# Batch 0's second feature half moves to the end of round two in a cross-attention and SERF feed-forward kernel

## The chip, the cores and the metric

The kernel runs on one core of one Trainium2 chip. Its time is the device time in microseconds (us) of one execution. Before the change, three runs took 704.97, 705.04 and 706.51 us; the median is 705.04 us. Besides these runs there is one profiled execution, with a record of each instruction on each engine.

The engines are named as in the profile: PE is TensorE (matrix products), PEld its loading of stationary operands, DVE is VectorE, ACT is ScalarE, POOL is GpSimd, and SP is SyncE, which only issues transfers here. A name such as SPq or POOLq is the DMA queue of that engine. "ACT copy" or "DVE copy" below means a copy of a result from PSUM, where TensorE leaves it, to SBUF.

## The reference, cut to what matters

```python
B, H, S, Ns, D = 8, 8, 512, 32, 64          # x: (B, H, S, D), state: (B, H, Ns, D)
d_model, d_ff = 512, 2048

scores  = x @ state^T / sqrt(D);  a  = softmax(scores)     # (B, H, S, Ns)
xread   = a @ state                                        # each token reads the states
scores2 = state @ x^T / sqrt(D);  a2 = softmax(scores2)    # (B, H, Ns, S)
sread   = a2 @ x                                           # each state reads the tokens
rows    = concat([xread, sread], axis=2) -> (B * (S + Ns), H * D) = (4352, 512)

h   = rows @ w_in                                          # w_in  (512, 2048)
g   = h * erf(softplus(h))
out = g @ w_out                                            # w_out (2048, 512)
```

The inputs x and state are float32. The two weight matrices arrive as float64; the chip sees them as pairs of 32-bit words, and the kernel makes float32 of them with two passes on ScalarE and three instructions on VectorE for each piece.

## The kernel before, in words

**Features and batches.** The 2048 features of d_ff are 16 blocks of 128; four blocks are a group, so there are four groups, and two groups are a feature half. Half 0 is groups 0 and 1, half 1 is groups 2 and 3. A batch has 512 token rows (four tiles of 128 rows) and 32 state rows.

**Mixed product.** Since xread is a times state, the first layer is computed as a times (state @ w_in). The product state @ w_in of a batch for one group is called mixed here: `mixed_part` (L600, products in L613) for batch 0, `mixed` (L1130, products in L1138) for the others. Its results are copied from PSUM to tiles named `m`.

**Batch 0 with plain products.** At the start, only batch 0 is worked on, while the weights arrive. It goes through all four groups with ordinary products: `first` (L617, product L624) makes h, `second` (L626, product L631) accumulates the output rows in four PSUM banks over all 16 blocks. Softplus and erf run on ScalarE (L661, L664), the multiplication by h on VectorE (L666). The weights come from SP's queue in pieces (`weight`, L140): w_in pieces of two blocks and w_out pieces of two blocks, 1 MB of float64 each, 8 of each matrix. They go through a ring of three buffers named `raw`, and are converted by ScalarE (L167, L169) and VectorE (L172, L173, L174). Pieces of w_in for half 1 are laid in a part of `ring` and stored to DRAM (`kept_in`) from there by `kept`. The order of all these steps is a list written out by hand, `order0` (L758), with the steps' short names: p201 is the second product of group 2, row tile 0, block 1; i4v0 is the first VectorE step of w_in's piece 4. `lead` and `warm` (L191, L193) put products whose result is not used ahead of others.

**Strassen products for the other batches.** Batches 1 to 7 use products of Strassen's kind with seven multiplications in place of eight. `first_product` (L1223, product L1237) makes h for one half: two column parts of seven products, 14 in all, each of four records in the profile. `serf` (L1267) does softplus and erf on ScalarE and the multiplication on VectorE (L1277). `sums_a` (L1284, L1288) makes sums of blocks of g, and `sums_w` (L1299, L429) differences of blocks of w_out, four instructions for a half. `second_product` (L1308, L1321) multiplies them by seven products. `twice_product` (L1411, product L1508) applies the scheme at two levels, 49 products of four records; `sums_b` (L1367, L1383) makes its weight sums. `sums_y` (L1170) makes the sums of attention weights that the first product needs; `keep_y` and `bring_y` store them in DRAM and bring them back.

**Rounds.** Round one makes half 0 of batches 1 to 7, with `second_product` for batches 1 to 5 and `twice_product` for 6 and 7, and writes the partial output rows. In it the attention of the following batches is computed (`attend` L980, `read` L1089, `turn_read` L1112). State rows of all batches are done together (`first_states`, `second_states`). Round two makes half 1 of batches 1 to 7 with `twice_product`, and adds to the rows already in DRAM by accumulating transfers on GpSimd's queue (L1556). The very last unit (half 1 of batch 7) instead reads the stored rows back into tiles, adds its blocks to them in SBUF (`join`, L1568) and stores the sums from SP's queue (`store`, L1572).

**The weights between the rounds.** The weight sums of half 1 (`sums_w(1, ...)`) are made in batch 2's unit of round one. `keep_w` (L1403) then stores w_out's half 1 and its three sums in DRAM, four transfers on SP's queue, since `sums_b` for half 0 is going to overwrite them before batch 6; `bring_w` brings them back before round two.

**What sets the order.** From batch 1 on, each instruction or short series of instructions is an `op` (L796) with its engine, a planned cost, a planned time, and the regions that it reads and writes. `ORDER` fixes for each engine the order of its ops. `emit` (L919) goes through them on the plan's clock and issues them; `in_order` (L82) then ties each engine to that order. So every engine, and every queue so tied, runs its list strictly in order: an instruction that waits holds up all that follow on its engine. In part one `in_order` covers TensorE, VectorE, ScalarE and SP; from batch 1 on, TensorE, VectorE and ScalarE.

## Time and profile before

| | |
|---|---|
| median of three runs | 705.04 us |
| span of the profiled execution | 702.9 us |
| TensorE busy | 694.6 us (99%) |
| VectorE busy | 571.8 us (81%) |
| ScalarE busy | 469.3 us (67%) |
| GpSimd busy | 58.9 us (8%) |
| granted TensorE clock | 1.00 in each window read below |
| bytes moved by DMA | 85.54 MB, mean 122 GB/s |

The span runs from the first to the last event of the profiled execution on the core. It lies 2.1 us under the median of the three runs; what is outside the span is not in the trace. A busy time is the sum over an engine's instructions, without overlap counted twice. In the lists of groups, a row names line, engine, operation, output and input tiles and the number of records, then the busy time and the mean duration in ns of one record. Successive records overlap a little, so the distance from one start to the next is shorter than the mean duration. A float32 matrix product appears in the profile as two records for each weight block, so 64 plain products of L631 for batch 0 (4 row tiles by 16 blocks) are 128 records. In the rows of waits, the figures are the total time waited, the number of waits, and the longest, in us.

### The profile page before, as it was taken

The page shows a single profiled execution, that of the slowest core. Times are in us where ns is not written, and L with a number is a line of the kernel's source. Part 1 is how long each engine was busy: PE and PEld are TensorE (multiplying, and loading weights), DVE is VectorE, ACT ScalarE, POOL GpSimd, SP SyncE. Part 2 cuts the span into 40 slices and gives each one's busy share as a digit, 9 for nine tenths or more (in the row PEclk, how much of TensorE's full clock was granted, in tenths as well). Part 3 has the DMA queues.
Part 4 walks back from the last instruction along what each step waited for, and adds up shares of the span by engine and source line. Part 5 has one row for each costly group of instructions (what it writes and reads, how often), then busy time and mean ns, then how long its engine had stood idle before and what let it go on. Part 6 is the DMA issues. An engine that isn't in the chain of part 4 may idle for free.

```text
span 702.9 us, 12986 instructions
## 1 busy us (share of the span) xinstructions
PE 694.6 (99%) x5039; PEld 565.4 (80%) x5039; DVE 571.8 (81%) x930; ACT 469.3 (67%) x812; POOL 58.9 (8%) x54
## 2 busy tenths in 40 slices
PE   8999999999999999999999999999999999999997
PEld 7444346687878778787999998798989898989997
DVE  6997887999979788696969753896979587778997
ACT  5999898949576655838473455846585756666842
POOL 0000000000000000000001000102021221212322
PEclk9999999999999999999999999999999999999999
DMA  8869582845648746352234514405152663435665
GB/s 261 260 194 252 191 192 46 201 86 108 179 85 259 198 81 201 55 173 53 93 98 120 161 58 165 98 31 96 17 98 33 111 75 69 60 42 65 104 94 106
DMA packets 159886, 85.54 MB, mean 122 GB/s; under 512 B 123728, under 2 KB 149328, under 8 KB 159056
## 3 DMA queue, kind: packets, MB, share of 16 engines
q1 hardware_dynamic: 146224, 71.59, 36.5%
q0 software_dynamic: 13056, 12.59, 14.3%
q8 instruction: 40, 0.66, 0.4%
q10 hardware_dynamic: 544, 0.52, 0.2%
q14 instruction: 22, 0.18, 0.1%
HBM read 46.27 MB, written 34.73 MB: 115 GB/s over the span
## 4 chain that ended last, share of the span: by engine, by line
PE 94%; DVE 4%; issue 0%; ACT 0%; DVEq 0%; ACTq 0%
PE o L1508 28%; PE o L1321 17%; PE h L1237 17%; PE o L631 8%; PE at L1237 7%; PE o L1725 3%; PE h L1676 3%; PE h L624 2%; PE at L624 2%; PE h L1138 2%; PE at L1138 2%; PE at L1676 1%; PE at L1100 1%; PE h L997 1%; PE at L613 1%; DVE ring L1568 1%
## 5 line engine op out<-in xcount | busy, mean ns | idle before, releaser
L1249 ACT COPY ring<-h 128x512 f32<-128x512 f32 x112 | 64.7, 586 | 84.3 <-PE h L1237 81.2
L1237 PE MATMUL h<-aT,m 128*128 128x256 f32 x336 | 85.1, 380 | 0.0
L1277 DVE TENSOR_TENSOR ring<-ring 128x1024 f32<-128x1024 f32 (+1 forms) x60 | 68.6, 1146 | 14.0 <-ACT ring L1274 13.4
L1321 PE MATMUL o<-w_out,ring 128*128 128x256 f32 x320 | 77.7, 383 | 0.0
L1321 PEld LDWEIGHTS o<-w_out,ring 128*128 128x128 f32 x320 | 59.6, 190 | 15.9 <-issue 5.9
L1259 ACT ACTIVATE ring<-ring 128x512 f32<-128x512 f32 x112 | 66.7, 631 | 6.6 <-PE o L1321 2.1
L1237 PEld LDWEIGHTS h<-aT,m 128*128 128x128 f32 x336 | 61.8, 190 | 10.4 <-ACT ring L1249 0.8
L1288 DVE TENSOR_TENSOR ring<-ring 128x1024 f32<-128x1024 f32 x56 | 67.8, 1217 | 0.3
L631 PE MATMUL o<-w_out,ring 128*128 128x512 f32 x128 | 59.7, 599 | 0.0
L1508 PE MATMUL o<-w_out,w_in 128*128 128x128 f32 x448 | 59.6, 275 | 0.0
L1274 ACT ACTIVATE ring<-ring 128x1024 f32<-128x1024 f32 (+1 forms) x60 | 59.0, 1004 | 0.2
L1321 PE MATMUL o<-raw,ring 128*128 128x256 f32 x240 | 58.9, 381 | 0.1
L1508 PE MATMUL o<-w_out,ring 128*128 128x128 f32 x432 | 58.8, 276 | 0.0
L1508 PEld LDWEIGHTS o<-w_out,ring 128*128 128x128 f32 x432 | 54.1, 192 | 4.2 <-issue 1.7
L1508 PEld LDWEIGHTS o<-w_out,w_in 128*128 128x128 f32 x448 | 56.0, 192 | 1.7 <-issue 0.8
L1556 POOL DMA_DIRECT2D out_dram<-oo x14 | 17.0, 1213 | 448.5 <-ACT o L1529 360.8
L1321 PEld LDWEIGHTS o<-raw,ring 128*128 128x128 f32 x240 | 45.3, 190 | 9.5 <-issue 2.5
L631 PEld LDWEIGHTS o<-w_out,ring 128*128 128x128 f32 x128 | 23.7, 190 | 27.6 <-issue 26.2
L1508 PE MATMUL o<-raw,ring 128*128 128x128 f32 x324 | 44.7, 276 | 0.0
L1508 PEld LDWEIGHTS o<-raw,ring 128*128 128x128 f32 x324 | 41.3, 192 | 2.4 <-issue 1.7
L1251 DVE TENSOR_TENSOR ring<-ring,at 128x512 f32<-128x512 f32 x28 | 19.1, 684 | 23.5 <-ACT ring L1249 21.8
L1508 PE MATMUL o<-raw,xT 128*128 128x128 f32 x288 | 37.3, 275 | 0.0
(289 smaller groups left out, 1391.5 us busy)
## 6 DMA issues: line engine op xcount, KB each, us to landing
raw<-in_moe_w_in_dram SPq DMA_DIRECT2D x16, 512.0 KB, 4.8
raw<-in_moe_w_out_dram SPq DMA_DIRECT2D x8, 1024.0 KB, 5.3
xq<-in_x_dram SPq DMA_DIRECT2D x112, 64.0 KB, 2.5
x<-in_x_dram SPq DMA_DIRECT2D x56, 128.0 KB, 3.2
out_dram<-oo SPq DMA_DIRECT2D x10, 512.0 KB, 3.7
kept_a<-aT SPq DMA_DIRECT2D x7, 512.0 KB, 3.2
aT<-kept_a SPq DMA_DIRECT2D x7, 512.0 KB, 4.6
out_dram<-oo POOLq DMA_DIRECT2D x14, 256.0 KB, 4.4
```

The source lines that it names most:

```text
L624: nc.tensor.matmul(out=h_t[g, i], lhsT=m_t[0, g][:, e, P * i:P * i + P], rhs=aT[0][:, e], start=start, stop=not start)
L631: nc.tensor.matmul(out=acc[r], lhsT=gT[g][:, i, P * r:P * r + P], rhs=w_out[:, GF * g + i, :], start=(made_of[r] == 1), stop=(made_of[r] = ...
L1138: nc.tensor.matmul(out=bank(names[e])[q, :], lhsT=st[r, b, q], rhs=of_group[2 * u + j][r, :, i, :], start=True, stop=True)
L1237: nc.tensor.matmul(out=out_[:, i], lhsT=x_[:, q:q + P], rhs=y_, start=(start and i == 0), stop=(i == 1), skip_group_check=not start)
L1249: op(ACT, 0.5, t, lambda: nc.scalar.copy(out_(), view(bank(name))), [name], w)
L1259: op(ACT, 0.53, t, lambda: nc.scalar.activation(out=part(splane, k), in_=part(hplane, k), func=ACTF.Softplus), area(hplane, ks=[k], os=[o] ...
L1274: op(ACT, 0.085 + 0.875 * share, at + n, lambda s_=s_: nc.scalar.activation(out=s_, in_=s_, func=ACTF.Erf), [], area(splane, ks=[k], os=os ...
L1277: op(DVE, 0.065 + 1.075 * share, at + n + 1, lambda s_=s_, h_=h_: tt(s_, s_, h_, op=ALU.mult), area(hplane, ks=[k], os=os), area(splane, k ...
L1288: op(DVE, 1.14, at + k, lambda k=k, x_=x_, y_=y_, how=how: tt(get("h", k), get(*x_), get(*y_), op=how), area(v[x_[0]], ks=[x_[1]]) + area( ...
L1321: nc.tensor.matmul(out=view(name)[:, h], lhsT=lhs[:, i, :], rhs=weight_of[n]()[:, u, i, :], start=(start and h == 0 and i == 0), stop=(h = ...
L1508: nc.tensor.matmul(out=out_[:, Q2 * k:Q2 * k + Q2], lhsT=lhs[:, k, i], rhs=rhs[:, i], start=first, stop=(k == len(ns) - 1 and i == 1), ski ...
L1676: nc.tensor.matmul(out=bank(bk)[:, P * i:P * i + P], lhsT=x_[:, i, k], rhs=y_[:, k], start=(start and i == 0 and k == 0), stop=(i == GF - ...
```

## The change

Batch 0 no longer does all of its features at the start.

1. **Only half 0 of batch 0 at the start.** Batch 0's steps become ops of the planner (`begin0`, `mixed0`, `first0`, `serf0`, `second0`, `put0`), for groups 0 and 1 only. `order0` and its helpers go. Batch 0's four partial row tiles are stored by `put0`, from GpSimd's queue.
2. **Half 1 of batch 0 as the last unit of round two.** Round two runs over batches 1 to 7 and then 0. The new last unit uses `first_product` and `twice_product` as the others do, with its own `sums_y`, `keep_y`, `bring_y` and `mixed`.
3. **Weights of half 1 staged in round one.** SP's queue fetches only the first eight pieces of 1 MB. The blocks of half 1 are fetched in 16 stages (`stage`), one block of 512 KB each, alternately of w_in and w_out, by GpSimd's queue into halves of the three `raw` buffers; each is converted with the same five instructions, half as wide. A converted block of w_in is stored to `kept_in`, by GpSimd's queue.
4. **Weight sums and their store.** `sums_w(1)` moves from batch 2's unit to that of batch 5 (`TWICE - 1`), and `keep_w` goes from SP's queue to GpSimd's.
5. **Copies.** Of batch 0's copies from PSUM, ten named in `BY_VECTOR` are on VectorE, and all others on ScalarE.
6. **The last block.** In the last unit, the output block whose products come last is no longer copied to a temporary and joined. Each of its results is added straight from PSUM to the tile that holds the rows read back (`into`), and the block is stored in three parts.
7. **Orders.** `ORDER` is new for all engines and also has GpSimd's and SP's queues for the whole kernel; `in_order` covers all five. The planned time of batch 1's first unit (`BASE`) is 66 in place of 24.

```diff
-    def in_order(begun, engines=(nc.tensor, nc.vector, nc.scalar, nc.sync)):
+    def in_order(begun, engines=(nc.tensor, nc.vector, nc.scalar, nc.sync, nc.gpsimd)):
...
+    BY_VECTOR = set("""
+        x2 st s01 m010 m011 m020 m021 u0 u1 m120""".split())
...
+    def spare_products(name, n, at):
+        op(PE, 0.112 * n, at, lambda: warm(bank(name)[:, 0:P], n), [], [name])
...
+            spare_products("o%d" % g, 3 if g else 14, 12.6 + 5 * g)
...
+    def fetch_in(f, k, h, at, late=False):
+        how, on = late_load if late else ((SP, 0.5), nc.sync)
+        op(*how, at, lambda: on.dma_start(
+            out=half(k, h).rearrange("p (a b) -> p a b", a=NK),
+            in_=moe_w_in[:, P * f:P * f + P].rearrange("(k p) f -> p k f", p=P).bitcast(U32)),
+           [("out0", 1)] * late, RAW(k, [h]), land=9.0 * late, pipe=1.42 * (not late))
+
+    late_load = (GP, 2.0), nc.gpsimd
+
+    def fetch_out(f, k, h, at):
+        op(GP, 1.4, at, lambda: nc.gpsimd.dma_start(
+            out=half(k, h), in_=moe_w_out[P * f:P * f + P].bitcast(U32)),
+           [("out0", 1)], RAW(k, [h]), land=8.0)
...
+    def second0(g, r, i, at):
+
+        def go():
+            made_of[r] += 1
+            nc.tensor.matmul(out=bank("o%d" % r), lhsT=gT[g][:, i, P * r:P * r + P],
+                             rhs=w_out[:, GF * g + i, :], start=(made_of[r] == 1),
+                             stop=(made_of[r] == NF // 2))
...
+    def put0(r, at):
...
+        op(ACT, 0.48, at, lambda: nc.scalar.copy(ot(), bank("o%d" % r)), [],
+           ["oacc%d" % r, "ot%d" % (r % 2)])
+        rows = out[0:S].rearrange("(p c) e -> c p e", p=P)
+        op(GP, 1.2, at + 1, lambda: nc.gpsimd.dma_start(out=rows[r], in_=ot()),
+           ["ot%d" % (r % 2)], [("out0", r)], land=4.0)
...
     def keep_w(at):
-        op(SP, 2.4, at, lambda: [nc.sync.dma_start(out=k, in_=t) for t, k in weights_of(1)],
+        op(GP, 5.6, at, lambda: [nc.gpsimd.dma_start(out=k, in_=t) for t, k in weights_of(1)],
+           W_of(1), ["kept_w"], land=18.0)
...
+            if final is not None and ns == (3,):
+                join_others()
+
+                def into(frm, h, q, t, region=region, of_bank=of_bank):
+                    to = mine(0, 1)[:, h, Q2 * q:Q2 * q + Q2]
+                    op(DVE, 0.2, t, lambda: tt(to, to, region[frm](), op=ALU.add),
+                       [of_bank[frm]], area(final, us=[0], ks=[2 + h], os=[q]))
+
+                copy = add = into
...
-            join(0, 1, R3, at + 22)
-            store(0, 1, at + 22)
...
+        if final is not None:
+            for h, qs in (1, slice(0, 2)), (0, slice(0, 1)), (0, slice(1, 2)):
+                cols = slice(Q2 * qs.start, Q2 * qs.stop)
+                op(SP, 0.4, at + 26, lambda h=h, cols=cols: nc.sync.dma_start(
+                    out=quad(0, 1)[:, h, cols], in_=mine(0, 1)[:, h, cols]),
+                   area(final, us=[0], ks=[2 + h], os=range(qs.start, qs.stop)), [], land=2.2)
+            return
...
-    U, BASE = 40.0, 24.0
+    U, BASE = 40.0, 66.0
...
+    def stage(n, at):
+        f, k, e = NF // 2 + n // 2, n % 3, n // 2 % 2
+        if n % 2:
+            fetch_out(f, k, 1, at)
+            convert(("o", f), half(k, 1), w_out[:, f], RAW(k, [1]), [("Wo", f)], at + 5)
+        else:
+            fetch_in(f, k, 1, at, True)
+            convert(("i", f), half(k, 1), mt(3)[:, e], RAW(k, [1]), [("mS", 1, e)], at + 5)
+            op(GP, 1.4, at + 10, lambda: nc.gpsimd.dma_start(
+                out=kept_in[:, f - NF // 2], in_=mt(3)[:, e]), [("mS", 1, e)],
+               [("kin", f - NF // 2)], land=6.0)
+
+    for n in range(NF):
+        stage(n, BASE + 8 + 8 * n)
...
-            if b == 2:
-                sums_w(1, base + 20, 1, 2, 4, 3)
-                keep_w(base + 30)
+            if b == TWICE - 1:
+                sums_w(1, base + 5, 1, 2, 4, 3)
+                keep_w(base + 12)
...
+    turns = [*range(1, B), 0]
...
     emit()
-    in_order(begun, [nc.tensor, nc.vector, nc.scalar])
+    in_order(begun)
```

## The prediction

> **What bounds the kernel now.** I read the page's engine totals first, then its slices, its chain of waits, the list of what TensorE (PE) waited for, and a table of 20 us windows.
>
> ```profile
> span 702.9 us, 12986 instructions
> PE 694.6 (99%) x5039; PEld 565.4 (80%) x5039; DVE 571.8 (81%) x930; ACT 469.3 (67%) x812; POOL 58.9 (8%) x54
> PE   8999999999999999999999999999999999999997
> DVE  6997887999979788696969753896979587778997
> PE 94%; DVE 4%; issue 0%; ACT 0%; DVEq 0%; ACTq 0%
> PE o L531 <- DVE ring L553: 1.1, 1, 1.1
> PE o L193 <- PEq L1915: 0.8, 1, 0.8
> PE at L1113 <- ACT sT L1116: 0.7, 1, 0.7
> PE o L485 <- DMA x<-in_x_dram: 0.4, 1, 0.4
> PE h L613 <- DVE w_in L174: 0.4, 1, 0.4
> PE at L1138 <- DVE ring L1255: 0.2, 1, 0.2
> 20.00:40.00 20.00, 20.00 (x82) 8.73 (x82) 18.78 (x29) 19.87 (x24) 0.00 (x0) 1.00 0.75 214
> 140.00:160.00 20.00, 20.00 (x163) 16.42 (x162) 18.98 (x32) 9.87 (x19) 0.00 (x0) 1.00 0.52 93
> ```
>
> TensorE is the bound: 99% busy, 94% of the chain, and its six waits sum to 3.6 us, all before 140 us. The granted clock is 1.00 in every window, so only TensorE's work and its waits can move the time. VectorE (DVE) is the engine that comes next: in the windows its column (the third busy one) reads 18.78 and 18.98 of 20. So a change that takes TensorE's work out of the start may find VectorE there.
>
> **What leaves TensorE.** Groups 2 and 3 of batch 0 go, which were plain products.
>
> ```profile
> 27.78 10.30 PE o L631 x24
> 19.21 3.52 PE h L624 x8
> 135.82 6.04 PE o L1321 x28
> 357.37 2.68 PE o L1508 x24
> 168.59 1.02 PE h L1138 x16
> ```
>
> These pieces of the chain give the pace: 10.30/24 = 0.429 us for a record at L631, 3.52/8 = 0.44 at L624 (0.43 in the longer runs), 6.04/28 = 0.216 for a 256-wide one, 2.68/24 = 0.112 at L1508, 1.02 for a mixed product. Half of L631's 128 records is 64 x 0.429 = 27.5; 32 of L624's 64 at 0.43 are 13.7; four mixed products of 0.6 are 2.4. That is 43.6 us away. The new unit adds 14 first products of 4 records (56 x 0.216 = 12.1), 49 two-level ones of 4 (196 x 0.112 = 21.9) and two mixed (2.0): 36.0. TensorE is relieved of 7.6 us.
>
> **The end.** In the timeline before, TensorE ends at 698.26, the last sum in L1523 runs to 698.89, and the join in L1568 from 698.99 to 699.68; then the store lands. Adding straight from PSUM leaves the join out: 0.8 us. The three stores instead of one can cost this again (0 to 0.8); I take 0.8, since the stores' issues lie on an empty SP queue.
>
> So the span is 702.9 - 3.6 - 7.6 - 0.8 + L = 690.9 + L, where L is all the time that TensorE will wait. The profiled execution's span lies 2.1 us under the median of the runs, 705.04, so the time is 693.0 + L. It breaks even at L = 12.
>
> **L: what VectorE has to do before the first Strassen products.** I lay the new order out by rows. A conversion of a piece is L172, L173, L174: their starts lie 0.60, 1.14 and 1.14 apart, 2.9 in all; a half piece 1.5. Other 512-wide instructions start 0.60 apart, 1024-wide ones 1.15. The first multiplication (L1277) that batch 1's second product needs is the 127th instruction in VectorE's new order; the 126 ahead are: 7 whole pieces, the first in two parts and three staged halves (27.8), attention of batches 1 and 2 (33 instructions, 19.0), batch 0's softmax (8.5), 8 multiplications L666 (4.8), four weight sums (4.6), copies from PSUM (3.9), sums of L1170 (2.7), mixed sums (2.4), three multiplications (1.8), two additions (1.2): 76.7. VectorE first has data at 5.9 (its wait for L485), so 82.6. TensorE's work ahead of the same product: warm-up and lead products 8.9 (22 leads at 3.39/14 = 0.24), attention 12.3, mixed 2.6 + 2.0, first products of batch 0 13.8, second 31 x 0.858 = 26.6, batch 1's first 12 x 0.863 = 10.4, from 0.8: 77.4. The gap is 5.2; the same account at batch 3's second product gives 5.4, and it closes after about 240 us.
>
> On top of it: VectorE's idle time at the head, where scores, the 14 leads and the softmax stand in one row. Before, 0-20 us had 6.7 idle, 0.8 beyond the first 5.9; walking the new order, 3.7. I take 3.0, near the upper end, since fewer conversions are at hand to fill it. Then gaps between instructions: the best window before was 97% busy (19.42 of 20), 3% of 77 is 2.3. Against it, my TensorE prices sum to 678.3 for the whole new queue where 694.6 - 7.6 = 687.0 is due, 1.3%, 1.0 at this place. L = 5.2 + 3.0 + 2.3 - 1.0 = 9.5, and the time 702.5; the case spans 700 to 706 (L 7 to 13: no idle at the head below, gaps up to batch 3 above).
>
> **What I cost at nothing, and its cover.** ScalarE (ACT): 8 conversions of 2 x 1.05 go (16.8) and table loads fall from 28 to about 15 (13 x 1.28), while some 5 us of copies and 1.2 per staged half come; it was 87% busy to 143 us and gets less. SP's queue loses 12 loads of weights, and the 2 stores of kept_in, 4 of keep_w and 4 of batch 0's rows go to GpSimd (POOL) or are replaced there: nothing on SP is later. GpSimd gets 16 loads, 8 stores, 4 of keep_w, 4 of rows: 32 issues at 1.20 to 1.46 us (its rows at L1556), 38 to 47 us in some 150 that were empty. Without that room each would delay the next load. The 16 staged conversions (1.5 each on VectorE, about 75 to 205 us) stand for 8 whole ones (23.2) that were done before 105 us; those that fall before the place in question are in the sum. The weight sums for half 1 (4 x 1.15) move from batch 2 to batch 5, as much work as before; keep_w must have landed before sums_b overwrites: VectorE has 22.7 us of work between. On SP keep_w took 6.6 to 8.1; GpSimd's 256 KB took 4.4 where SP's took 2.2, so 8.1 to 16.2: hidden. Behind it on GpSimd's queue wait only accumulating stores of outputs, which TensorE does not need. The extra unit in round two runs at VectorE's 80%.
>
> **A rule on GpSimd's loads.** While VectorE was 19.01 of 20 busy (680 to 700), GpSimd's issues stayed at 1.20 to 1.46 us. Only L172-like instructions (0.60) could stand in a load's way. The Trainium skill, page SBUF — State Buffer, section SBUF: two separate sides, says that such a load needs descriptors that GpSimd writes, and that it is locked out while VectorE runs a two-port instruction; it measures 620 ns growing to 3100. By this each staged load would be some 2.5 us later, an estimate from that page; hidden again while stages are 8 us apart. The trace here shows no such growth.
>
> **Rivals.**
> *VectorE idles as before* (slower). In its first 100 us it was busy 82.7, so 11.4 idle after the 5.9. It waited there for ScalarE's erf results (L666, 5.7) and copies (L1251, 2.7) and for products (L613, 3.5). If the new order keeps all of it, L = 5.2 + 11.4 - 1.0 = 15.6, 708.6 us. It decides from L = 14.1, that is 9.9 us of idle before batch 1's second product. Against it: fewer table loads on ScalarE and copies taken off VectorE's list.
> *A staged weight is late.* Conversions stand at fixed places in VectorE's order, so a piece not landed stops the multiplications behind it and TensorE after them. Loads on GpSimd's queue stand behind stores of kept_in that wait for VectorE. One whole landing of 5.8 us at VectorE's head gives L = 15.3, 708.3 us. Three buffers and 8 us a stage speak against it.
> *VectorE keeps up.* TensorE's own pace hides the gap (b1's products interleaved with batch 0's): L 4 to 7, say 5.5, 698.5 us. For it: TensorE waited 3.6 only before, with VectorE at 95%.
> *The unit is not cheaper.* If the last unit waits for its own sums, as no other unit follows to fill TensorE, the 7.6 is gone in part: 3 to 5 us, 706. The last unit before had no such wait (20.00 in every window to 680, 18.24 in the last).
>
> **How the numbers follow.** No change is within 0.3%, 2.1 us, about what can be told here: 702.9 to 707.2. My case (702.5): 0.55, of it 0.30 below 702.9 and 0.25 within. VectorE keeps up: 0.10, faster. VectorE idles: 0.20, slower. A late weight: 0.10, of it 0.07 slower. Unit not cheaper: 0.05, within. Faster 0.40, same 0.33, slower 0.27. My case's own range is 700 to 706; for 8 in 10 with both signs I take 698 to 709.
>
> **What would show it.** TensorE busy about 687; L1508 records 196 more, L631's half. TensorE's waits sum to about 9.5, nearly all before 160 us and on VectorE's L1277-like multiplications or on first-product sums, not on a DMA. VectorE over 93% busy from 20 to 160 us. In the tail no 0.69 join after the last product. Wrong: a long wait of VectorE for raw from GpSimd's queue, waits of TensorE after 240 us, or VectorE under 88% in the first 100 us while TensorE waits.

## The result, and the profile after

The changed kernel took 723.13 us (median of four runs, 719.11 to 726.7) beside 705.0 before: a ratio of 1.025, with a 95% interval of 1.021 to 1.029. It is slower by 18 us where 702.5 was forecast, and lies outside the range of 698 to 709. The profiled execution is the shortest of the four, with a span of 717.3 us. Its trace thus explains 14.4 us of the difference; what the longer executions add is taken up with the experiments. A run over 1.5% above the fastest run of its kernel is left out of the ratios; there is one, the longest of the kernel with ten leads at the head.

The page of the changed kernel: the engines' totals, TensorE's granted clock in 40 slices, and the chain of waits.

```profile
PE 698.8 (97%) x5163; PEld 581.6 (81%) x5163; DVE 593.4 (83%) x989; ACT 471.9 (66%) x850; POOL 85.7 (12%) x93
PEclk9899998999999999999999999999999999999999
PE 82%; DVE 4%; SPq 4%; DMA 1%; ACT 1%; issue 1%; DVEq 0%; ACTq 0%
```

TensorE's share of the chain has fallen from 94 to 82%, and SP's queue and the DMA, which had no place in it, have come in. The granted clock has two dents, in slices 2 and 7. These are the waits of TensorE over 1.1 us: what waited and its line, for what, us in total, times, longest.

```profile
PE h L684 <- DVE xq L676: 3.6, 1, 3.6
PE h L580 <- ACT m L161: 2.1, 1, 2.1
PE at L114 <- POOL ident masks.py:199: 1.4, 1, 1.4
PE o L1003 <- DVE ring L959: 1.3, 1, 1.3
PE o L438 <- DVE ring L463: 1.3, 1, 1.3
PE h L820 <- ACT ring L931: 1.2, 1, 1.2
```

And four windows of it around the two dents: from and to, length, busy time of TensorE, its weight loads, VectorE, ScalarE and GpSimd with their instructions, the granted clock, the DMA share and GB/s.

```profile
20.00:24.00 4.00, 2.75 (x9) 1.86 (x10) 3.86 (x10) 3.26 (x7) 0.00 (x0) 0.50 0.59 105
24.00:28.00 4.00, 4.00 (x22) 1.38 (x20) 3.84 (x6) 3.98 (x6) 0.00 (x0) 0.68 0.37 88
104.00:108.00 4.00, 1.59 (x12) 0.76 (x16) 2.40 (x5) 0.00 (x0) 0.00 (x0) 0.63 0.91 198
108.00:112.00 4.00, 4.00 (x20) 2.13 (x7) 3.74 (x8) 2.43 (x5) 0.55 (x1) 0.51 0.64 123
```

All waits of TensorE sum to 12.9 us (3.6 before). Its busy time is 698.8 us (694.6 before), and the time behind its last product 5.2 (4.6 before): these three make up 14.1 of the 14.4 us. The granted clock is 0.50 to 0.68 in these four windows; it was 1.00 in each that the prediction read. Summed over windows of 2 us, busy time times the missing part of the clock is 5.4 us; this work at half speed is part of the busy time.

The largest wait, L684, is that of the scores of batch 3 for its tokens (`xq`). The chain of waits (start, length) shows what it hung on; L93 is the load of xq.

```profile
89.15 5.76 SPq L93
...
95.58 2.90 SPq L93
...
102.84 2.56 DMA xq<-in_x_dram
...
105.60 0.72 DVE xq L676
106.32 0.09 issue
106.41 3.07 PE h L684 x16
```

SP's rows of the timeline show its list up to there (start, length; L768 loads x, L754 transfers the attention weights; two stores lie between them and xq):

```profile
62.56 10.47 SPq L768 DMA_DIRECT2D x<-in_x_dram  x8
73.13 11.46 SPq L754 DMA_DIRECT2D sc<-xT  x16
...
85.81 17.52 SPq L93 DMA_DIRECT2D xq<-in_x_dram  x16
```

And GpSimd's rows of the same timeline, with its idle time before and what ended it in brackets:

```profile
85.43 0.55 POOL L533 DMA_DIRECT2D raw<-in_moe_w_out_dram  x1 [21.16 <-DVE m L550]
86.49 1.09 POOL L1529 DMA_DIRECT2D kept_in<-m  x2 [0.51 <-DVE m L550]
87.58 0.54 POOL L657 DMA_DIRECT2D out_dram<-ot  x1
88.11 0.76 POOL L525 DMA_DIRECT2D raw<-in_moe_w_in_dram  x1
88.86 0.54 POOL L533 DMA_DIRECT2D raw<-in_moe_w_out_dram  x1
90.17 0.55 POOL L657 DMA_DIRECT2D out_dram<-ot  x1 [0.77 <-ACT ot L654]
```

SP's list had no idle stretch from 53 to 118 us; 4.8 us of this time are waits of x's transfers (L768) until TensorE is done with the tokens before. The 16 transfers of xq took 17.52 us to issue, with 5.76 and 2.90 us in two single issues; the same 16 took 10.70 before. SP's rows of the kernel before at that place in its list:

```profile
98.55 4.34 SPq L76 DMA_DIRECT2D x<-in_x_dram  x8
110.60 10.57 SPq L361 DMA_DIRECT2D sc<-xT  x16
...
123.41 10.70 SPq L105 DMA_DIRECT2D xq<-in_x_dram  x16
```

There the list stood idle from 103 to 111 us. In the changed kernel GpSimd let out seven transfers in just the stretch of the 17.52 us, 2.5 MB (three loads and two stores of rows at 512 and 256 KB, two stores of `kept_in` at 256 KB), after it had stood 21 us for VectorE to free a buffer.

The tail, from the timeline: TensorE's last products, VectorE's last sum, and SP's last stores.

```profile
711.40 0.68 PE L1239 MATMUL o<-w_out,w_in 128*128 128x128 f32 x4
712.22 0.48 DVE L1264 TENSOR_TENSOR ring<-ring,o 128x128 f32<-128x128 f32 x2
712.11 1.24 SPq L1175 DMA_DIRECT2D out_dram<-ring  x2
713.39 1.10 SPq L1288 DMA_DIRECT2D out_dram<-ring  x2
```

From TensorE's end to the end of the span are 5.2 us, where 4.6 were measured before and 3.8 forecast. The join is gone, but the last stores stand on SP's list behind two others that are ready at the same moment.

### The profile page after: what moved, and what is told of

The parts are those of the page before. It is cut to its first block, busy times and chain, and to the rows that moved or that the text cites. A ratio compares the mean times of both kernels' runs of the same rounds, so it can differ in the third digit from the quotient of the medians.

```text
span 717.3 us, 13372 instructions
## 1 busy us (share of the span) xinstructions
PE 698.8 (97%) x5163; PEld 581.6 (81%) x5163; DVE 593.4 (83%) x989; ACT 471.9 (66%) x850; POOL 85.7 (12%) x93
## 4 chain that ended last, share of the span: by engine, by line
PE 82%; DVE 4%; SPq 4%; DMA 1%; ACT 1%; issue 1%; DVEq 0%; ACTq 0%
PE o L1239 30%; PE h L919 17%; PE o L1003 15%; PE at L919 7%; PE o L1422 3%; PE h L1373 3%; SPq L93 2%; PE h L820 2%; PE at L820 2%; SPq L754 1%; PE h L684 1%; PE at L1373 1%; PE at L782 1%; DVE ring L970 1%; PE o L622 1%
## 5 line engine op out<-in xcount | busy, mean ns | idle before, releaser
L919 PE MATMUL h<-aT,m 128*128 128x256 f32 x360 | 92.1, 382 | 0.1
L941 ACT ACTIVATE ring<-ring 128x512 f32<-128x512 f32 x120 | 72.3, 631 | 10.9 <-PE o L1003 2.6
L1003 PE MATMUL o<-w_out,ring 128*128 128x256 f32 x320 | 77.6, 383 | 1.3 <-DVE ring L959 1.3
L1003 PEld LDWEIGHTS o<-w_out,ring 128*128 128x128 f32 x320 | 60.1, 191 | 16.5 <-issue 3.0
L1239 PE MATMUL o<-w_out,w_in 128*128 128x128 f32 x512 | 69.2, 276 | 0.0
L1239 PEld LDWEIGHTS o<-w_out,w_in 128*128 128x128 f32 x512 | 64.5, 192 | 1.9 <-issue 0.3
L1239 PE MATMUL o<-w_out,ring 128*128 128x128 f32 x480 | 65.1, 276 | 0.0
L1239 PEld LDWEIGHTS o<-w_out,ring 128*128 128x128 f32 x480 | 60.5, 192 | 4.3 <-issue 0.8
L1159 POOL DMA_DIRECT2D out_dram<-oo x16 | 24.4, 1585 | 151.1 <-ACT ring L956 115.0
L1239 PEld LDWEIGHTS o<-raw,xT 128*128 128x128 f32 x320 | 38.8, 192 | 2.1 <-ACT o L1270 1.7
L622 PE MATMUL o<-w_out,ring 128*128 128x512 f32 x64 | 31.0, 607 | 0.1
L919 PE MATMUL at<-sy,sx 128*128 128x256 f32 x120 | 31.0, 381 | 0.0
```

The costliest lines, as they stand in the source:

```text
L622: nc.tensor.matmul(out=bank("o%d" % r), lhsT=gT[g][:, i, P * r:P * r + P], rhs=w_out[:, GF * g + i, :], start=(made_of[r] == 1), stop=(mad ...
L919: nc.tensor.matmul(out=out_[:, i], lhsT=x_[:, q:q + P], rhs=y_, start=(start and i == 0), stop=(i == 1), skip_group_check=not start)
L941: op(ACT, 0.53, t, lambda: nc.scalar.activation(out=part(splane, k), in_=part(hplane, k), func=ACTF.Softplus), area(hplane, ks=[k], os=[o] ...
L1003: nc.tensor.matmul(out=view(name)[:, h], lhsT=lhs[:, i, :], rhs=weight_of[n]()[:, u, i, :], start=(start and h == 0 and i == 0), stop=(h = ...
L1159: op(GP, 1.2, t, lambda: nc.gpsimd.dma_start(out=quad(r, c), in_=one(v), accum_op=ALU.add), every(*v), [("out", b, r, c)], land=6.0)
L1239: nc.tensor.matmul(out=out_[:, Q2 * k:Q2 * k + Q2], lhsT=lhs[:, k, i], rhs=rhs[:, i], start=first, stop=(k == len(ns) - 1 and i == 1), ski ...
```

## The experiments

Ratios are to the kernel before on the same chip, each with its 95% interval; its median was 704.84 to 704.95 us on each of these chips. A figure in us as measured is the median of a kernel's runs, and a wait or a clock is that of its one trace. Theory A in what follows: GpSimd's staged transfers collide with SP's, SP's list in strict order passes the delay on, and TensorE's waits bring its clock down.

**Quarter of the staged loads.**

```diff
-            out=half(k, h).rearrange("p (a b) -> p a b", a=NK),
+            out=half(k, h).rearrange("p (a b) -> p a b", a=NK)[:, 0:1 if late else NK],
...
-            out=half(k, h), in_=moe_w_out[P * f:P * f + P].bitcast(U32)),
+            out=half(k, h)[:, 0:d_model // 2],
+            in_=moe_w_out[P * f:P * f + P, 0:d_model // 4].bitcast(U32)),
```

> Each of the 16 staged weight loads moves a quarter of its bytes (128 KB in place of 512 KB); the order, the waits and the conversions stay, so half 1 of the weights is not what it should be. Theory A (the transfers collide): at 85 to 96 us GpSimd's loads and stores fill the DMA engines and SP's issue of batch 3's xq is held (one issue took 5.76 us, another 2.90), VectorE's transpose and TensorE's scores wait, and the clock halves behind it. It expects the 16 issues to take about 10.5 us in place of 17.5, TensorE's wait of 3.6 us at the scores and the second halving of the clock to be gone, and 6 to 9 us less. Theory B (VectorE's and SP's own lists are too long there, whatever the load): the wait stays at 3 to 4 us and the time within 2 us.

Measured: 713.57 us, 1.0119 (1.0104 to 1.0134), 9.6 less than the changed kernel. Each staged load moves a quarter of its bytes here. SP's row of the timeline:

```profile
82.21 12.71 SPq L93 DMA_DIRECT2D xq<-in_x_dram  x16
```

And the two windows of the second dent:

```profile
104.00:108.00 4.00, 4.00 (x20) 3.54 (x19) 3.97 (x10) 3.40 (x7) 0.27 (x1) 1.00 0.50 115
108.00:112.00 4.00, 4.00 (x20) 3.21 (x18) 3.90 (x6) 3.43 (x6) 0.00 (x0) 1.00 0.28 45
```

The 16 issues took 12.71 us, not quite the 10.5 that was expected, and TensorE does not wait for xq. The bytes of the staged loads, not their order or their conversions, made the wait at 103 us and the second dent. The wait of 1.2 us at 257 us of the changed kernel stands here at 250 us with 2.2, and a clock down behind it.

**No staged conversions.** The three VectorE instructions and the second ScalarE pass of the staged conversions are left out.

```diff
+        short = len(key) == 2 and words.shape[1] < 2 * 2 * d_model
...
-        op(DVE, 0.6 if full else 0.35, at + 0.6, lambda: nc.vector.tensor_scalar(
+        op(DVE, 0.6 if full else 0.35, at + 0.6, lambda: short or nc.vector.tensor_scalar(
...
-        op(ACT, 1.05 if full else 0.6, at + 0.5, lambda: nc.scalar.activation(
+        op(ACT, 1.05 if full else 0.6, at + 0.5, lambda: short or nc.scalar.activation(
...
-        op(DVE, 1.15 if full else 0.6, at + 1, lambda: tt(d, d, lo, op=ALU.add),
+        op(DVE, 1.15 if full else 0.6, at + 1, lambda: short or tt(d, d, lo, op=ALU.add),
...
-        op(DVE, 1.15 if full else 0.6, at + 2, lambda: nc.vector.scalar_tensor_tensor(
+        op(DVE, 1.15 if full else 0.6, at + 2, lambda: short or nc.vector.scalar_tensor_tensor(
```

> The three VectorE instructions and the second ScalarE pass of each of the 16 staged conversions are left out (so half 1 of the weights is not what it should be); loads and stores stay. It takes 24.5 us of VectorE and 9.6 us of ScalarE from 75 to 210 us. Theory A (transfers): the wait for batch 3's xq stays, VectorE has 4.6 us less before batch 1's second product, 2 to 5 us less time in all. Theory B (VectorE bounds the whole start): the lag falls by all that TensorE waits for there, 8 us or more.

Measured: 719.76 us, 1.0204 (1.0187 to 1.0221), 3.4 less in the median, with runs that overlap, for 24 us of VectorE's work. Of TensorE's waits in this kernel the longest is new, and the chain of waits shows what it hung on:

```profile
PE at L784 <- DMA sc<-xT: 8.3, 1, 8.3
```

```profile
84.09 9.50 DMA sc<-xT
```

TensorE now waits 8.3 us for the attention weights of batch 1, which SP issues from 73.27 to 85.55. The last of these transfers took 9.50 us to land, where the median of them took 2.6: GpSimd let out three staged loads, two stores of `kept_in` and one of rows from 81 to 85 us, and the DMA share read 0.92 and 1.06 in the two windows from 82 to 86 us. So the collision came back at another transfer. The wait for batch 3's xq, which theory A expected to stay, is gone. The gain is within the 2 to 5 us of theory A, and VectorE's sum alone does not bound the start.

**The staged loads on SP's queue.**

```diff
-    late_load = (GP, 2.0), nc.gpsimd
+    late_load = (GP, 2.0), nc.sync
...
-        op(GP, 1.4, at, lambda: nc.gpsimd.dma_start(
+        op(GP, 1.4, at, lambda: nc.sync.dma_start(
```

> The 16 staged loads go out from SP's queue in place of GpSimd's, at the place in the list that the plan's clock gives them; all else as in the changed kernel. Theory A (what hurts is the load on the DMA engines, and SP's list in strict order with it): no better, since the same bytes move at the same time and SP's list gets 16 more entries that wait for VectorE to free a buffer; 0 to 20 us slower than the changed kernel, 720 to 740. Theory C (GpSimd's own queue is slow, as its descriptors are): the loads land sooner and 3 us or more are won, below 719.

Measured: 723.15 us, 1.0258 (1.0238 to 1.0277), as the changed kernel. The long waits moved (6.1 us for VectorE's L933, ending at 177 us, and 3.8 for ScalarE at about 88), none was won. The equal time is made of two things. The staged loads went out at other times, xq's 16 issues took 13.04 us, and TensorE did not wait for xq at 103 us. In exchange a staged load stood on SP's list behind the 16 transfers of a later xq until 166.7 us; ScalarE waited 7.0 us for it to land, and VectorE 6.2 us for ScalarE. From issue to landing, the median of the staged w_out loads is 5.2 us in place of 6.0. So GpSimd's queue as such is not what costs the 18 us, but how much a queue of its own is worth is not shown.

**A burst in the kernel before.** The collision by itself, in two kernels.

```diff
+    def burst():
+        for k in range(5):
+            nc.gpsimd.dma_start(out=spare[:, k], in_=aT[1].rearrange("p e s -> p (e s)"))
```

> The kernel before, with five more stores on GpSimd's queue: batch 1's attention weights (512 KB, five times, 2.6 MB) to a spare tensor in DRAM as soon as they are made, at about 120 us, beside SP's 16 transfers of batch 3's xq, whose issues took 10.70 us. Nothing reads the copies. Theory A (transfers collide, and that alone slows SP's list): the 16 issues take 14 to 18 us. If the kernel before has room in SP's list there, as its idle stretch of 14 us before them suggests, the time stays within 1 us of 705; if not, up to 4 us more. Otherwise: issues at 10.5 to 11 us.

Measured: 705.94 us, 1.0018 (1.0008 to 1.0027). The five stores went out at 107.9 us, not at 120, and did not meet xq, whose issues took 10.36 us. The attention weights, issued from 111 us on, took 12.51 us in place of 10.57. In the second kernel the five copies of 512 KB go from DRAM to DRAM: they read the stored weights, and so start when that store has landed.

```diff
+            nc.gpsimd.dma_start(out=spare[:, k], in_=kept_a[1].rearrange("p e s -> p (e s)"))
...
+    op(GP, 6.0, 0, burst, ["kept1"], [])
```

> The kernel before, with five copies of 512 KB on GpSimd's queue from the store of batch 1's attention weights to a spare tensor, DRAM to DRAM, which can start when that store has landed, at 126 to 127 us, beside SP's 16 transfers of batch 3's xq (10.4 to 10.7 us for the issues). If colliding transfers alone slow SP's issue, it takes 14 us or more, as in the changed kernel (17.5 with 2.6 MB beside it). The time: as before within 1 us where SP's list has room, 2 to 5 us more where not. If they do not collide, 10.4 to 11 us.

Measured: 712.04 us, 1.0103 (1.0086 to 1.012). GpSimd's and SP's rows of the timeline:

```profile
124.44 2.78 POOL L1903 DMA_DIRECT2D spare<-kept_a  x5 [123.14 <-DMA kept_a<-aT]
```

```profile
124.13 16.46 SPq L105 DMA_DIRECT2D xq<-in_x_dram  x16
```

And TensorE's longest wait:

```profile
PE at L1100 <- DMA m<-xT: 2.6, 1, 2.6
```

With 2.5 MB beside them the 16 issues took 16.46 us where they took 10.70. This was passed on along SP's list to the attention weights behind them, for which TensorE waited 2.6 us; the clock then read 0.82 and 0.76 in the two windows of 4 us after 156 us. One burst cost the kernel before, with its idle stretches on SP's list, 7.2 us: more than the expected 2 to 5. So added transfers alone, with order and work as before, slow SP's list and TensorE behind it.

**Rows of half 0 from GpSimd's queue.** The wait of 1.2 us at L820 (257 us) had the same shape: SP's store of a row block (L1023) stood behind xq of batch 7, whose 16 issues took 18.09 us beside `keep_w`'s 3.5 MB on GpSimd's queue, and ScalarE waited 3.2 us for its landing.

```diff
-            op(SP, 0.4, t, lambda: nc.sync.dma_start(out=rows[r], in_=oo()[:, r]),
+            op(SP, 0.4, t, lambda: nc.gpsimd.dma_start(out=rows[r], in_=oo()[:, r]),
```

> The stores of half 0's rows of batches 1 to 5 (512 KB each) go out from GpSimd's queue in place of SP's, where one stood at 251 us behind the 16 transfers of batch 7's xq (18.1 us for the issues) and 8 of x, with ScalarE waiting 3.2 us for its landing and TensorE 1.25. Theory A: this wait is gone, 1 to 2 us less (3 to 5 in executions where the clock halves there); the wait at 103 us stays. Otherwise: unchanged within 1 us.

Measured: 718.2 us (717.19 to 718.35), 1.0185 (1.0168 to 1.0202). There is no wait of TensorE from 230 to 300 us. The median is 4.9 lower, and the runs differ by 1.2 us where those of the changed kernel differ by 7.6. Three of the other kernels with SP's list as in the change (spare products in the wait, order of the head, short conversion, all told below) had, in their profiled executions of 722.2 to 726.0 us, a further wait of 4.0 to 4.4 us at about 175 us: for a VectorE multiplication that stands on VectorE's list behind the transposition of a later xq. This xq landed late, issued behind two row stores and beside three staged transfers. That the longer runs of the changed kernel have this wait too is likely, but they left no trace.

**All of it small.** Staged loads a quarter, the store and fetch between the rounds a quarter, rows from GpSimd's queue; of these edits, that of the store:

```diff
...
-        op(GP, 5.6, at, lambda: [nc.gpsimd.dma_start(out=k, in_=t) for t, k in weights_of(1)],
+        op(GP, 5.6, at, lambda: [nc.gpsimd.dma_start(out=k[:, 0:k.shape[-1] // 4],
+                                                     in_=t[:, 0:t.shape[-1] // 4])
+                                 for t, k in weights_of(1)],
...
```

> All that collides is made small or taken off SP's list: staged weight loads a quarter, the store and the fetch of half 1's weights between the rounds (keep_w, bring_w) a quarter, and half 0's rows of batches 1 to 5 go out from GpSimd's queue; so half 1 of the weights is not what it should be. Theory A (the collisions and what hangs on them): no wait of TensorE over 1.5 us after 30 us and no halved clock there; what is left is the head with its halved clock (7 us), VectorE's lag before 91 us (6) and the tail (1.4): 708 to 711 us. Theory B (another cause after 100 us): 713 or more.

Measured: 710.31 us, 1.0076 (1.0061 to 1.0091), within the expected 708 to 711. Its longest waits:

```profile
PE h L582 <- ACT m L161: 2.1, 1, 2.1
PE at L114 <- POOL ident masks.py:199: 1.4, 1, 1.4
PE o L438 <- DVE ring L463: 1.3, 1, 1.3
```

All three lie in the first 23 us. So 12.8 of the 18 us are the transfers and what hangs on them. Counting TensorE's records one by one shows where: against the same record of the changed kernel this one is 0.3 us ahead at 97 us, 8.2 at 107.5 (115.7 there), and 9.7 at 354. Nearly all is won at the one wait for xq with its clock, and the rest after 230 us, where the wait at 257 us lay. This kernel still is 5.4 us slower than before. Its waits are 7.1 us (3.6 before), all of them ahead of 110 us, its halved clock costs 2.8, and its tail is 0.6 us longer.

**Spare products in the wait for the scores.**

```diff
+    op(PE, 0.24 * 14, 0, lambda: warm(bank("h0")[:, 0:P], 14), [], [])
```

> Fourteen spare products (3.4 us) stand ahead of batch 3's scores, where TensorE waits 3.6 us for its xq. They cost nothing if they run in the wait. Theory A (a wait of TensorE of this length brings the clock down to 0.50 for some 6 us): the clock stays at 1.00 at 105 to 112 us and 2.5 to 3 us are won. Theory B (the clock comes down for another reason): clock 0.50 there as before, no gain.

```profile
104.00:108.00 4.00, 3.43 (x31) 2.45 (x33) 2.13 (x4) 0.13 (x1) 0.00 (x0) 1.00 0.89 188
108.00:112.00 4.00, 4.00 (x25) 2.83 (x16) 3.93 (x8) 3.02 (x6) 0.55 (x1) 1.00 0.81 190
```

The wait at the scores fell to 0.6 us and the clock stayed at 1.00: the idle time is what brought it down. The whole took 726.0 us, 1.0302 (1.0277 to 1.0328), so the 2.5 to 3 us that were expected were not kept. The wait of 4.0 us at 175 us was there, for xq of a later batch. Holding TensorE busy does not bring the transfers sooner.

**The head.** Three kernels for the wait of 2.1 us at 17 us. Ten leads in it:

```diff
-            spare_products("o%d" % g, 3 if g else 14, 12.6 + 5 * g)
+            spare_products("o%d" % g, 13 if g else 14, 12.6 + 5 * g)
```

> Ten more lead products (2.4 us) stand on TensorE where it now waits 2.1 us at 17 to 19 us for ScalarE's copy. Theory A (the clock halves because TensorE stood idle): the granted clock stays at 1.00 from 20 to 27 us, where it was 0.50, and the work there takes some 3 us less; the later work gives back what VectorE cannot follow, so 1 to 3 us of the whole. Theory B (the clock does not follow this idle time): clock 0.50 as before and no gain, or 0.5 us lost.

Measured: 722.31 us, 1.0227 (1.0185 to 1.0269). Its runs go from 718.07 to 729.33 us, and the trace is that of the longest. In it the next wait (L438) grew from 1.3 to 1.7 us, and behind it the clock came down at 22 us, for 3.4 us in place of 6.8. So the two theories were not told apart. Then the old order of the head (the order lists of TensorE, ScalarE and VectorE, in this order: on VectorE the sum, inverse and scaling of the first half ahead of the second half's maximum, on ScalarE the copies of the first mixed product ahead of the second exponential):

```diff
-            8 0 5 1-3 6 15 9 4 7 10 12 16 13 17 11 14 18 ...
+            8 0 5 1 2 3 6 15 9 4 7 10 12 16 17 11 13 14 18 ...
...
-            0-3 5 14-15 4 12-13 7 6 8 16 10 17 32-33 18-19 55 ...
+            0 1 2 3 5 14 15 4 12 13 7 6 8 16 32 33 10 17 18 19 55 ...
...
-            1 0 2 77 16 3 17 4 18 13-15 8-9 5 19 6-7 10 78-79 11-12 41 40 ...
+            1 0 2 77 16 3 17 4 18 13 14 15 5 6 7 8 9 78 79 10 11 12 19 41 40 ...
...
-            spare_products("o%d" % g, 3 if g else 14, 12.6 + 5 * g)
+            spare_products("o%d" % g, 8 if g else 14, 12.6 + 5 * g)
```

> Only the order of the first 23 VectorE instructions, four of ScalarE and one set of lead products is changed: batch 0's second maximum, its exponential and the first halves of the other maxima come after the sum, the inverse and the scaling of the first half, as in the kernel before, and eight leads stand ahead of the second turn. Expected: the first product of batch 0 (L597) starts at about 21 us in place of 23.2, and TensorE has no wait of over 1.5 us before 30 us. If the halving of the clock at 20 to 27 us comes from such a wait, it goes too, and 30 us into the kernel 5 us are won. Theory A (SP's chain of transfers sets the pace from 53 us on, and starts when batch 1's scores are done): the chain starts as much earlier, so 3 to 5 us of the whole are kept. Theory B (VectorE's sum of work sets it): 0.5 us or less.

Measured: 728.09 us, 1.031 (1.0262 to 1.0358). The first product began at 22.8 in place of 23.2, not 21: ScalarE's copies of the attention weights (L161) now came late, 1.65 us. The expectation failed. Last, both waits filled, with rows on GpSimd's queue:

```diff
-            spare_products("o%d" % g, 3 if g else 14, 12.6 + 5 * g)
+            spare_products("o%d" % g, 11 if g else 14, 12.6 + 5 * g)
...
+    op(PE, 0.24 * 7, 0, lambda: warm(bank("o1")[:, 0:P], 7), [], [])
...
-            op(SP, 0.4, t, lambda: nc.sync.dma_start(out=rows[r], in_=oo()[:, r]),
+            op(SP, 0.4, t, lambda: nc.gpsimd.dma_start(out=rows[r], in_=oo()[:, r]),
```

> The kernel with half 0's rows from GpSimd's queue (718.2), and 15 more spare products at the head: 8 where TensorE waits 2.1 us for ScalarE's copy at 17 us, 7 ahead of the second turn where it waits 1.2. If the waits bring the clock down, it stays at 1.00 from 19 to 28 us, the first products of batch 0 end 2.7 us sooner, and 0.5 to 3 us of the whole are kept, 715 to 717.7; if the lag is made good by the waits for SP's transfers at 103 us, nothing is kept.

```profile
20.00:24.00 4.00, 3.82 (x22) 2.62 (x21) 3.86 (x9) 3.78 (x8) 0.00 (x0) 1.00 0.53 77
24.00:28.00 4.00, 3.05 (x24) 1.06 (x22) 3.84 (x7) 3.97 (x5) 0.00 (x0) 1.00 0.56 156
```

Measured: 716.87 us, 1.0166 (1.0149 to 1.0182); 1.3 less than the 718.2 without it, with runs that overlap. The clock stays up, and six records of L597's first products take 2.84 us in place of 4.42. But TensorE then waits 1.5 us more for VectorE's copies at 28 us. Record for record, it is 2.5 us ahead of the kernel without the leads at 24 us, and 0.8 us at 60 us and at 96.

**VectorE and ScalarE before 91 us.** In every kernel so far batch 1's second product began at 90 to 92 us, or later. Three kernels relieve the engines ahead of it. In the first, the third VectorE instruction of the whole conversions at the start is left out.

```diff
+        short = words.shape[1] == 2 * 2 * d_model
...
-        op(DVE, 1.15 if full else 0.6, at + 2, lambda: nc.vector.scalar_tensor_tensor(
+        op(DVE, 1.15 if full else 0.6, at + 2, lambda: short or nc.vector.scalar_tensor_tensor(
```

> The changed kernel, with the third VectorE instruction (sign bits) of the seven whole conversions at the start left out (so the weights lose their signs): 8 us of VectorE's work before 65 us. The products, transfers and their order stay. Theory V (VectorE's list bounds the start to 91 us): batch 1's second product starts at 85 to 88 us in place of 91.0. Theory A (SP's chain bounds from 53 us on): it starts at 90 to 91, and the time stays within 1.5 us of the changed kernel's.

Measured: 723.69 us, 1.0259 (1.024 to 1.0279); the product began at 90.47. Eight us off VectorE's list won nothing alone. Then this line together with all lines of the small moves:

> The kernel with the small moves (quarter of the staged loads and of half 1's weights, rows of half 0 from GpSimd's queue), and also without the third VectorE instruction of the seven first whole conversions; so the weights are not what they should be. If VectorE's list and SP's chain bound the start to 91 us in turn, batch 1's second product now starts at 85 to 88 us and the time falls below the 710.3 of the small moves alone by 2 to 5 us. If neither does (the products before it are late from the head on), it starts at 90 again and the time stays within 1 us of 710.

Measured: 709.62 us, 1.0067 (1.005 to 1.0084), with the product at 89.8: 0.7 us less than with small moves alone, with runs that overlap, for SP's list and VectorE's both being relieved. Last, on the kernel with small moves, ScalarE's second pass and VectorE's addition of the low bits left out of the same conversions:

```diff
-        op(ACT, 1.05 if full else 0.6, at + 0.5, lambda: nc.scalar.activation(
+        op(ACT, 1.05 if full else 0.6, at + 0.5, lambda: short or nc.scalar.activation(
...
-        op(DVE, 1.15 if full else 0.6, at + 1, lambda: tt(d, d, lo, op=ALU.add),
+        op(DVE, 1.15 if full else 0.6, at + 1, lambda: short or tt(d, d, lo, op=ALU.add),
```

> The kernel with the small moves (710.3 us), and the second ScalarE pass and the second VectorE instruction (the low bits) of the seven first whole conversions left out: 7.4 us of ScalarE and 8.0 of VectorE before 60 us, so the weights lack their last three bits besides. The kernel with small moves and 8.0 us less on VectorE alone took 709.6 and began batch 1's second product at 89.8. If ScalarE's list bounds 24 to 60 us, the second product starts at 83 to 87 us and the time is 704 to 707. If not, it starts at 89 to 90 again and the time is 709 to 710.

Measured: 707.99 us, 1.0048 (1.0033 to 1.0063), with the product at 88.4. Windows of the kernel with small moves, and then of this one:

```profile
24.00:60.00 36.00, 34.75 (x151) 13.27 (x150) 34.59 (x50) 34.80 (x42) 0.00 (x0) 0.96 0.66 157
```

```profile
24.00:60.00 36.00, 35.86 (x184) 14.58 (x186) 28.14 (x45) 30.93 (x40) 1.06 (x2) 0.98 0.69 167
```

ScalarE (the fourth busy column) was busy 34.80 of 36 us, 97%. With 7.4 us off its list and 8.0 off VectorE's, the kernel gains 2.3 us; 8.0 off VectorE's alone gained 0.7. So some 1.6 us hang on ScalarE's list, and record for record 0.6 of them are won by 26 us and most of the rest by 40. No kernel relieves ScalarE alone, so how much it bounds by itself is not shown. The time falls between the two outcomes that were expected: the rest of the lag, some 3 us of the 5.4, is not settled.

**The last stores.**

```diff
-                op(SP, 0.4, at + 26, lambda h=h, cols=cols: nc.sync.dma_start(
+                on = nc.sync if h else nc.scalar
+                op(SP, 0.4, at + 26, lambda h=h, cols=cols, on=on: on.dma_start(
```

> The last two of the three stores of the last block go out from ScalarE's queue in place of SP's. In the changed kernel they were issued at 713.39 behind two other stores at 712.11, 0.7 us after the last sum. Expected: 0.5 to 1.2 us less between TensorE's last product and the end (5.2 us now); nothing else moves, so the time is within 1 us of the changed kernel's.

Measured: 721.56 us, 1.0253 (1.0204 to 1.0301). From TensorE's end to the end of the span are 4.7 us in place of 5.2. The half microsecond is at the lower edge of what was expected, and less than the runs of this kernel differ by.

None of these kernels beats the one before.

## Why the prediction was wrong

*TensorE's work falls by 7.6 us; break-even at L = 12.* With this frame, L is read as 717.3 - 690.9 = 26.4 us. Of this, 12.9 are the listed waits, 5.4 the halved clock, for which the prediction had no term, and 1.4 the tail (5.2 where 3.8 was put in). The remaining 6.7 says that the fall itself did not come. TensorE was busy 698.8 us, not about 687; without the 5.4 of halved clock that is 693.4, 1.2 less than before. Even in the kernel with small moves it is 692.4 (695.2 less 2.8), 2.2 less than before. The numbers of records are those that were forecast (196 more of the two-level products, half as many second products), so what is off is their pace, and why is not settled.

*The gap of VectorE at batch 1's second product.* I put TensorE there at 77.4 us, 1.0 more for my prices, and 9.5 us of waiting on top, 87.9. It came at 90.97.

```profile
90.97 1.13 PE L1003 MATMUL o<-w_out,ring 128*128 128x256 f32 x4
```

That is 3.1 us later, and the first halved clock is about 2.7 (2.75 x 0.50 + 4.00 x 0.32 from the windows). That the size was nearly right is in part luck. TensorE was idle 7.1 us up to there, not the 10.3 of the sum (0.8 and 9.5), and busy 83.9; without the 2.7 of clock that is 81.2, where 77.6 was priced (76.6 and 1.0). And the reason given was not right: taking 8 us from VectorE won half a microsecond there, and taking the load off ScalarE and SP's list as well won 2.5.

*"ScalarE ... was 87% busy to 143 us and gets less."* An average again. From 24 to 60 us it was 35.06 of 36 us busy before, and gets only 0.6 less, 34.48: 5.8 us of conversions go there, but it has one table load more (9 in place of 8) and takes over copies. Up to 143 us the table loads fell from 28 to 20, not to about 15.

*"SP's queue loses 12 loads ...: nothing on SP is later."* This is the step that failed. I counted what SP issues, not when, and took GpSimd's 32 transfers for issues of 1.2 to 1.5 us on an empty queue without their load on the DMA engines. In the kernel before SP's list had idle stretches, 103 to 111 us for one; in the changed one it has none from 53 to 118, and 7 us lost in it reach TensorE. It is worth 12.8 us of the 18 by the kernel with small moves, and the burst in the kernel before shows the same chain by itself.

*The rival "a staged weight is late".* Its mechanism came near, for another transfer: the weights were in time (nothing waits for a staged one), and the tokens that SP loads beside them were late. Its price, 708.3 us, is 14.8 short.

*The rule on GpSimd's descriptors.* The rows that I set against it were of accumulating stores; these are the loads, by the page's groups of the changed kernel, with busy time and mean ns of one:

```profile
L525 POOL DMA_DIRECT2D raw<-in_moe_w_in_dram x8 | 6.1, 765 | 35.5 <-ACT m L542 12.3 <-ACT m L826 11.7 <-ACT ring L931 10.1
L533 POOL DMA_DIRECT2D raw<-in_moe_w_out_dram x8 | 4.3, 544 | 62.2 <-DVE m L550 21.2 <-ACT ring L931 21.1 <-ACT m L826 17.2
```

Beside a VectorE that was 94% busy from 60 to 200 us they took 0.54 to 0.77 us, at most 0.79. So a growth of these issues is not what cost the time. The accumulating stores of the outputs at the end did grow, from 1213 to 1585 ns in the mean for those from `oo`; why is not settled, and nothing of TensorE waits for them.

*keep_w "hidden".* It was, for the sums that wait for it. Its 3.5 MB delayed xq of batch 7 (18.09 us) and through it a store and ScalarE.

*The tail: 0.8 us less.* It became 0.6 more than before. The bound "three stores can cost this again" was the right one to take: "an empty SP queue" was not empty.

*VectorE idles as before* did not happen: it was busy 87.27 of the first 100 us (82.7 before), and its longest idle stretch from 7 us to 300 us was one of 4.9 us for xq, at 105. But 87.27 is under the 88 that the prediction named as a sign of being wrong. Another sign, a wait of TensorE after 240 us, came too; the third, a long wait of VectorE for `raw`, did not. *No waits after 240 us* was wrong by the one of 1.2 us at 257.

## What to carry to other kernels

A transfer moved to an idle queue is free for the queue, not for the DMA engines: lay its bytes beside what the other queues move in the same microseconds, and look for the list in strict order that has no gap left to take up the delay. Where work is cut from a stage, list all engines and queues of that stage alone; here TensorE, VectorE and ScalarE were 95 to 96% busy from 24 to 60 us and SP's list was full from 53, and relieving one alone won 3.4 us at most. A wait of TensorE of 2 us or more is priced with the halved clock behind it, here 1.5 to 3.3 us on top.

## What the runs showed of the hardware

Behind every single wait of TensorE of 2.0 us or more (2.0 to 8.3 us, in the fourteen kernels that had one) the granted clock went to 0.50; behind single waits up to 1.5 us it never did, and behind 1.6 to 1.9 us in some executions and not in others. Each time it stayed down for 3.4 or 6.8 us (3.41 to 3.42 or 6.82 to 6.83, by windows of half a microsecond), so each such wait cost 1.5 to 3.3 us more. The Trainium skill, page TensorE: Matmul & The Clock Gate, section Part 1: The HAM clock gate (the "warmup" mystery), has a clock of two values, whole and half, decided anew in windows of about 3.4 us that run freely. The two values and the time that it stays down agree with these rows. That it takes at least one idle window of that length doesn't: 2 us sufficed here (2.03 us of idle time at 262 us in the kernel with 8 us off VectorE's list, with TensorE busy without a gap from 256 us up to it), and the measurement decides.

An issue on SP's queue that takes 0.49 us on its own took 5.76 us in the changed kernel's collision, with the DMA share at 1.02 and 1.07 from 88 to 96 us, and 4.09 us in that of the burst, with the share at 0.94 from 126 to 132 us. A full share alone does not do it: in the kernel before it read 1.01 to 1.07 from 86 to 92 us, and the longest of the 16 issues of xq there took 1.21 us. What holds the queue back is not shown.
